# Masks as matmuls, zero matmuls in waits, and new engine orders in a fused attention and channel-mix kernel

## The chip, the cores and the metric

The kernel runs on one core of one Trainium2 chip. The core has five engines: TensorE (PE, with its weight loads listed as PEld), VectorE (DVE), ScalarE (ACT), GpSimd (POOL) and SyncE (SP), which here issues nearly all DMAs. The metric is the device time of one execution in microseconds (us). Several executions of a kernel are timed and the median is taken.

## The reference

Inputs are q, k and v, each 4 batches x 8 heads x 768 positions x 64, in fp32, and the weights of a channel mix. First comes attention in which a query sees the first 4 positions (the sinks) and the last 128, itself included:

```python
scores = scale * q @ k.T
keep = (pos[None] < 4) | ((rel >= 0) & (rel < 128))    # rel = query position - key position
a = softmax(where(keep, scores, -1e9)); x = a @ v      # heads side by side: 512 wide
xk = mu_k * x + (1 - mu_k) * x_prev                    # x_prev: the position before
xr = mu_r * x + (1 - mu_r) * x_prev
out = sigmoid(xr @ w_r) * (relu(xk @ w_k) ** 2 @ w_v)
```

The channel mix follows: w_k is 512 x 1024, w_v 1024 x 512 and w_r 512 x 512. The output is 4 x 768 x 512 in fp32.

## The kernel before

The work is cut into 12 units, each 256 positions of one batch, so three units to a batch. A unit goes through four stages. `prepare` loads q, k and v, casts them to bf16, transposes q and k (on PE with a copy out of PSUM by ACT or DVE, for late units by DMA) and puts v beside a column of ones. `attend` multiplies keys by queries into one of two PSUM tiles called `sc`, takes the exponential on ACT into `e` (line 1092; for unit 0, line 805), multiplies `e` by a mask of zeros and ones on DVE (line 1106; for unit 0, line 818), multiplies by v on PE (lines 1125 and 831) and divides by the sum that the column of ones has made. The sinks, where they lie outside the unit's own keys, have scores and products of their own (lines 987, 1063 and 1078; 1078 is the form in quarter tiles and 1063 the plain one). `mix` transposes x and makes xk and xr on DVE (line 1220; for unit 0, line 907). `ffn` makes the keys (line 1275; for unit 0, line 930, since unit 0 goes in two halves of 128 positions), relu and square, the gate with w_r (line 1314, tanh in place of the sigmoid) and the product with w_v (line 1334). The weights come in fp32 and are cast in pieces: w_k in four, w_r in two, w_v in four (lines 629, 633 and 635).

Nothing of this is ordered by a loop. Each step is entered with `P.op` under a running number, with the keys that it reads and writes and the buffers that it takes or holds. `ORDER` lists the numbers for PE, DVE, ACT, POOL and SP, each engine in the order in which it is to work, and `CHOICE` says for steps that several engines can do which one does them. `Plan.schedule` walks the five lists with planned costs, hands out buffers (four PSUM banks called `bank`, two `sc` tiles, and so on) and puts out the instructions. An engine works through its own list in order; between engines, semaphores hold an instruction until its data is there. A step whose number stands behind another's on the same engine can't pass it.

Two further parts matter here. `Plan.fill` (line 1358) puts matmuls of zeros on PE where the plan sees a wait: over 600 ns in the first 4 us of the plan and over 300 ns after, up to a planned time of 22 us, into a free `bank`; they compute nothing that is used. And `BIAS` names units whose mask is added to the scores by a matmul (a bias of 0 or -30000, times the identity, started in PSUM ahead of the scores) instead of being multiplied on DVE. It is empty, and only the units after unit 0 have the code for it (`biased` in `attend`). The bias tiles would lie in the third output buffer, which is free early, beside the rows of mu. mu is transposed by one small matmul (`spread_mu`, line 614), entered ahead of all units.

Of the kernel before, what the change touches and what calls it, by code (L numbers as in the profile page):

```python
# [8 lines left out]
FP32 = mybir.dt.float32  # L9
# [9 lines left out]
    79: "POOL", 80: "ACT", 81: "ACT", 84: "ACT", 87: "ACT", 91: "DVE", 94: "DVE", 95:  # L19
    "DVE", 97: "DVE", 100: "DVE", 129: "POOL", 132: "DVE", 138: "POOL", 141: "DVE",  # L20
    142: "DVE", 160: "PE/tiles", 172: "PE/full", 177: "ACT", 189: "POOL", 192: "POOL",
    194: "DVE", 198: "DVE", 214: "ACT", 222: "ACT", 225: "DVE", 242: "PE/tiles", 254:
    "PE/full", 271: "POOL", 274: "POOL", 276: "DVE", 283: "DVE", 303: "ACT", 307:
    "ACT", 311: "ACT", 349: "POOL", 352: "DVE", 355: "POOL", 357: "DVE", 361: "DVE",
    381: "ACT", 389: "ACT", 405: "PE/full", 417: "PE/tiles", 433: "POOL", 435: "POOL",
    457: "ACT", 465: "ACT", 469: "ACT", 485: "PE/tiles", 495: "ACT", 497: "PE/full",
    508: "DVE", 510: "DVE", 513: "POOL", 524: "DVE", 540: "ACT", 548: "ACT", 581:
    "ACT", 587: "POOL", 592: "POOL", 594: "DVE", 598: "ACT", 600: "DVE", 616: "ACT",
    620: "ACT", 624: "ACT", 644: "PE/tiles", 656: "PE/full", 667: "POOL", 669: "DVE",
    676: "DVE", 685: "DVE", 698: "ACT", 706: "ACT", 722: "PE/tiles", 732: "ACT", 734:  # L30
    "PE/tiles", 745: "DVE", 749: "DVE", 751: "DVE", 781: "ACT", 808: "ACT", 814:
    "ACT", 819: "ACT", 822: "POOL", 824: "POOL", 826: "DVE", 845: "ACT", 848: "DVE",
    849: "ACT", 853: "ACT", 857: "ACT", 873: "PE/tiles", 883: "ACT", 885: "PE/full",
    890: "ACT", 896: "POOL", 898: "DVE", 902: "POOL", 904: "DVE", 905: "DVE", 925:
    "ACT", 929: "ACT", 933: "ACT", 949: "PE/tiles", 959: "ACT", 961: "PE/full", 980:
    "DVE", 1000: "DVE", 1001: "ACT", 1016: "DVE", 1025: "ACT",
# [7 lines left out]
BIAS = ()  # L44
# [12 lines left out]
FIRST = 0  # L57

# [39 lines left out]
    ),  # L98
    "DVE": (
# [23 lines left out]
    ),  # L123
    "ACT": (
# [15 lines left out]
    ),  # L140
    "POOL": (
# [3 lines left out]
    ),  # L145
# [1274 lines left out]
```

## Time and profile before

| | |
|---|---|
| three timed runs | 167.68, 169.44 and 171.79 us; median 169.44 |
| the profiled execution | 170.43 us, of which the span from first to last instruction is 167.5 |
| mean granted TensorE clock in it | 0.98 |
| DMA | 34.38 MB, mean 205 GB/s |

The profile is of one execution. Its page gives busy time by engine, the span in 40 slices, the chain of work that ended last, groups of instructions with the idle time before them, and DMA issues with the time to landing. Other views of the same trace are used below: busy time by stretches that one chooses (PE, PEld, DVE, ACT and POOL, then the granted clock, the DMA share and GB/s), and the timeline, whose rows have start, duration, engine, line, operation, out<-in, shapes and count, and in brackets the idle time ahead and what ended it. L930 is line 930 of the kernel before. Durations overlap a little when instructions of one engine follow each other, so start-to-start distances are shorter than durations.

### The profile page before, as it was taken

How to read it: one execution, taken by the hardware profiler on the slowest of the kernel's cores; microseconds unless marked ns; L12 is line 12 of the kernel's file. 1: busy time of each engine (PE TensorE's matmuls, PEld its weight loads, DVE VectorE, ACT ScalarE, POOL GpSimd, SP SyncE). 2: the span in 40 equal slices, each digit the busy share in tenths (PEclk: the TensorE clock that was granted, in tenths of full speed). 3: DMA queues.
4: the chain of work that ended last, by engine and by line, in shares of the span. 5: the costliest groups of instructions: out<-in, count | busy, mean ns of one | idle time of the engine just before them, and what ended most of it. 6: DMA issues, size and time to landing. Idle time of an engine off the chain costs nothing.

```text
span 167.5 us, 4800 instructions
## 1 busy us (share of the span) xinstructions
PE 154.5 (92%) x1872; PEld 104.3 (62%) x1890; DVE 145.9 (87%) x373; ACT 133.2 (80%) x246; POOL 36.7 (22%) x66
## 2 busy tenths in 40 slices
PE   6577769999999999999999999999988999999992
PEld 2336559765658676667666686855844774867441
DVE  6499997999899999999999999999949889897241
ACT  3577996999899998999999999799887698522411
POOL 5553202217206133055001320140131000000000
PEclk9997896999999999999999999999999999999999
DMA  4999999995989989999899988989997990302033
GB/s 120 242 306 379 331 304 345 386 388 158 223 245 283 193 214 281 200 210 164 211 178 232 223 197 111 265 155 150 266 136 165 219 224 0 129 0 114 11 129 121
DMA packets 73429, 34.38 MB, mean 205 GB/s; under 512 B 63800, under 2 KB 65088, under 8 KB 73408
## 3 DMA queue, kind: packets, MB, share of 16 engines
q1 hardware_dynamic: 73248, 34.02, 85.9%
q8 instruction: 14, 0.23, 0.6%
q10 hardware_dynamic: 160, 0.07, 0.1%
q14 instruction: 7, 0.06, 0.1%
HBM read 24.12 MB, written 6.29 MB: 182 GB/s over the span
## 4 chain that ended last, share of the span: by engine, by line
PE 68%; DVE 17%; DMA 8%; issue 2%; ACT 2%; SPq 1%; DVEq 0%
PE bank L1334 20%; PE bank L1275 18%; PE bank L1314 11%; PE bank L1125 6%; DMA xt<-x 5%; PE sc L1018 4%; DMA ks<-in_k_dram 3%; DVE e L1106 3%; PE bank L1182 2%; DVE xk L1220 2%; PE bank L706 2%; DVE xk L907 2%; DVE e L818 1%; DVE xr L1220 1%; SPq L476 1%
## 5 line engine op out<-in xcount | busy, mean ns | idle before, releaser
L1334 PE MATMUL bank<-wv_h,kk 128*128 128x512 bf16 x173 | 45.3, 379 | 1.4 <-DVE x L1143 0.8
L1275 PE MATMUL bank<-xk,wk_sb 128*128 128x256 bf16 x352 | 45.8, 273 | 0.2
L1092 ACT ACTIVATE e<-sc 128x1024 bf16<-128x1024 f32 (+1 forms) x44 | 41.5, 977 | 0.1
L1275 PEld LDWEIGHTS <-wk_sb 128*128 128x128 bf16 x352 | 32.8, 98 | 8.1 <-issue 0.9
L1106 DVE TENSOR_TENSOR e<-e,mask 128x1024 bf16<-128x1024 bf16 (+1 forms) x44 | 29.1, 678 | 0.6 <-ACT e L1092 0.6
L1285 ACT ACTIVATE rl<-bank 128x512 bf16<-128x512 f32 x41 | 23.5, 607 | 7.2 <-PE bank L1275 7.1
L1334 PEld LDWEIGHTS <-kk 128*128 128x128 bf16 x184 | 16.9, 98 | 16.1 <-issue 1.1
L744 POOL CAST vb<-vs 128x512 bf16<-128x512 f32 x18 | 14.4, 805 | 44.1 <-DMA vs<-in_v_dram 43.9
L1314 PE MATMUL bank<-wr_sb,xr 128*128 128x512 bf16 x89 | 23.7, 379 | 0.4
L1322 ACT ACTIVATE th<-bank 128x512 f32<-128x512 f32 x24 | 14.5, 613 | 9.5 <-PE bank L1314 9.5
L1220 DVE SCALAR_TENSOR_TENSOR xr<-td,mu_all,xt 128x256 bf16<-128x256 bf16 x44 | 21.8, 506 | 0.0
L1220 DVE SCALAR_TENSOR_TENSOR xk<-td,mu_all,xt 128x256 bf16<-128x256 bf16 x44 | 20.3, 492 | 0.2
L1345 DVE SCALAR_TENSOR_TENSOR ob<-th,bank 128x512 f32<-128x512 f32 x23 | 15.6, 681 | 4.7 <-PE bank L1334 3.1
L1125 PE MATMUL bank<-vb,e 128*128 128x65 bf16 x328 | 15.6, 197 | 0.3 <-DVE vb L744 0.2
L1125 PEld LDWEIGHTS <-e 128*128 128x128 bf16 x328 | 13.8, 100 | 3.1 <-issue 0.3
L1298 ACT ACTIVATE kk<-rl 128x512 bf16<-128x512 bf16 x25 | 15.4, 637 | 0.0
L1314 PEld LDWEIGHTS <-xr 128*128 128x128 bf16 x96 | 8.9, 98 | 9.2 <-issue 0.2
L1143 DVE TENSOR_TENSOR x<-bank,rec 128x256 bf16<-128x256 f32 x34 | 13.8, 415 | 0.4
L1209 DVE TENSOR_TENSOR td<-xt 128x512 bf16<-128x512 bf16 x22 | 9.5, 430 | 3.0 <-DMA xt<-x 2.7
L1018 PE MATMUL sc<-qt,kt 64*64 64x128 bf16 (+2 forms) x480 | 12.0, 229 | 0.0
L1152 ACT ACTIVATE x<-bank,rec 128x64 bf16<-128x64 f32 x40 | 9.2, 322 | 2.9 <-DVE rec L1139 2.8
L1018 PEld LDWEIGHTS <-kt 64*64 64x64 bf16 x480 | 8.7, 109 | 2.7 <-issue 1.5
(104 smaller groups left out, 194.5 us busy)
## 6 DMA issues: line engine op xcount, KB each, us to landing
vs<-in_v_dram SPq DMA_DIRECT2D x24, 256.0 KB, 4.5
out_dram<-ob SPq DMA_DIRECT2D x23, 256.0 KB, 3.0
ks<-in_k_dram SPq DMA_DIRECT2D x16, 256.0 KB, 4.5
qs<-in_q_dram SPq DMA_DIRECT2D x7, 512.0 KB, 5.8
qs<-in_q_dram SPq DMA_DIRECT2D x10, 256.0 KB, 4.5
ks<-in_k_dram SPq DMA_DIRECT2D x4, 512.0 KB, 10.0
w<-in_moe_w_k_dram SPq DMA_DIRECT2D x2, 1024.0 KB, 9.9
w<-in_moe_w_v_dram SPq DMA_DIRECT2D x2, 1024.0 KB, 9.5
```

The lines of the kernel that those rows point to most:

```text
L1018: nc.tensor.matmul(out=sc[keys, a, o0 + f0 - q0:o0 + f1 - q0], lhsT=lhs[rows, keys], rhs=qs[rows, f0:f1], start=u not in BIAS, stop=True, ...
L1092: nc.scalar.activation(out=buf[ek][:, :, lo:], in_=buf[sck][:, :, lo:], func=AF.Exp, scale=scale)
L1106: nc.vector.tensor_tensor(out=at, in0=at, in1=m, op=ALU.mult)
L1125: nc.tensor.matmul(out=o[:, g, a, :], lhsT=e[:, a, e0:e0 + 128], rhs=rhs, start=(T == 0 and i == 0), stop=(i == len(blocks) - 1), skip_gro ...
L1220: nc.vector.scalar_tensor_tensor(out=buf[key][:, c, :], in0=buf[tk][:, i, :], scalar=mu[w][:, c:c + 1], in1=xt[:, c, t0 - 1:t0 + 255], op0 ...
L1275: nc.tensor.matmul(out=ps[:, i, :], lhsT=wk_sb[:, c, 128 * f:128 * f + 128], rhs=xk[:, c, :], start=(c == 0), stop=(c == NC - 1), skip_gro ...
L1285: nc.scalar.activation(out=buf[rk], in_=buf[psk].rearrange("p (i t) -> p i t", i=2), func=AF.Relu)
L1298: nc.scalar.activation(out=buf["kk", u][:, 2 * f2:2 * f2 + 2, :], in_=buf[rk], func=AF.Square)
L1314: nc.tensor.matmul(out=buf[psk], lhsT=buf["xr", u][:, c, 128 * g:128 * g + 128], rhs=wr_sb[:, c, :], start=(c == 0), stop=(c == NC - 1))
L1322: P.op("ACT", act(512), lambda psk=psk, tk=tk: nc.scalar.activation(out=buf[tk], in_=buf[psk], func=AF.Tanh, scale=0.5), rank + 4 + g, tak ...
L1334: nc.tensor.matmul(out=buf[psk], rhs=wv_h[:, f, :], lhsT=buf["kk", u][:, f, 128 * g:128 * g + 128], start=(f == 0), stop=(f == NF - 1))
L1345: P.op("DVE", dve(512), lambda psk=psk, tk=tk, bk=bk: nc.vector.scalar_tensor_tensor(out=buf[bk], in0=buf[tk], scalar=1.0, in1=buf[psk], o ...
```

## The change

`BIAS` becomes `(0, 1)`: the masks of units 0 and 1 are added to their scores by matmuls, and `attend_first` gets the code for it (six matmuls 128x512 for unit 0; eight for unit 1 by the code that was there). POOL makes the two bias tiles. `spread_mu` and its copy are entered behind the scores of unit 0. The identity is kept in fp32 as a whole. The zero matmuls may now go into `sc` tiles and into the buffer that the waiting step itself has taken, and up to a planned time of 36 us. `CHOICE` and `ORDER` are new throughout: 14 matmuls are added on PE, and 13 zero matmuls stand where 5 stood. Of the 24 casts of v, POOL keeps 10 of 18, DVE has 6 for 5 and ACT 8 for 1; DVE has 10 relus for 4. In the order of loads q of unit 0 now leads k, and the first part of w_k goes ahead of q of unit 2, the second behind v of unit 1 and k of unit 2. `STRAIGHT`, a path without the cast, is empty, so its code makes no instruction.

```diff
-BIAS = ()
+BIAS = (0, 1)
...
-    ident8 = tile1([2 * NC, 2 * NC], FP32, "ident8")
+    ident32 = tile1([128, 128], FP32, "ident32")
+    ident8 = ident32[0:2 * NC, 0:2 * NC]
...
             if o["engine"] == "PE" and self.fill:
 
                 now = before
-                while t - now > (300.0 if now > 4000.0 else 600.0) and now < self.fill_until:
-                    some = [b for b in free["bank"] if b[0] <= now]
+                while now < self.fill_until:
+                    least = 300.0 if now > 4000.0 else 600.0
+                    some = [(max(b[0], now), k, name, b) for name in ("bank", "sc") for k, b in
+                            [(1, b) for b in free[name]] + [(0, b) for n, b in own if n == name]]
+                    some = [x for x in some if t - x[0] > least]
                     if not some:
                         break
...
+                    if u in BIAS:
+
+                        def biased(g=g, sk=sk):
+                            w = 128 * (g + 1)
+                            for a in range(2):
+                                nc.tensor.matmul(
+                                    out=buf[sk][:, a, :].rearrange("p (c w) -> p c w", w=w),
+                                    lhsT=ident, start=True, stop=False, skip_group_check=True,
+                                    rhs=bias[0][:, 128 * g:128 * g + w].unsqueeze(
+                                        1).to_broadcast([128, 512 // w, w]))
+
+                        P.op("PE", 430.0, biased, r, lag=PE_LAG, take=[("sc", sk)],
+                             reads=["ident", "bias0"], writes=[sk + ("b",)])
...
-                P.op("DVE", 2 * dve(width // 2, 0.52), masked, r, hold=[ek], port=True,
-                     writes=[part], reads=["mask0"])
+                if u not in BIAS:
+                    P.op("DVE", 2 * dve(width // 2, 0.52), masked, r, hold=[ek], port=True,
+                         writes=[part], reads=["mask0"])
...
+    def after_scores():
+        P.op("PE", 100.0, spread_mu, -40, lag=PE_LAG, take=[("bank", "mup")], mode=4,
+             reads=["ident", ("mu8", 0), ("mu8", 1), ("sc", 0, 0)], writes=["mup"])
+        P.op("DVE", 80.0, lambda: nc.vector.tensor_copy(out=mu_all, in_=buf["mup"][:, 0:2 * NC]), -40,
+             hold=["mup"], reads=["mup"], writes=[("mu", 0), ("mu", 1)])
...
-    P.fill_until = 22000.0
+    P.fill_until = 36000.0
```

More of the change, by code (lines that the diff above doesn't have):

```diff
@@ L18 @@
 CHOICE = {
[L19 to L36, printed above, removed]
+    79: "POOL", 80: "ACT", 81: "POOL", 82: "ACT", 84: "ACT", 87: "ACT", 89: "DVE", 91:
@@ new lines @@
+    "DVE", 92: "DVE", 98: "DVE", 100: "DVE", 102: "ACT", 127: "ACT", 130: "DVE", 132:
+    "DVE", 133: "POOL", 136: "POOL", 141: "DVE", 142: "DVE", 143: "DVE", 145: "DVE",
+    152: "DVE", 162: "PE/full", 173: "PE/full", 181: "ACT", 182: "DVE", 185: "POOL",
+    188: "POOL", 194: "ACT", 195: "DVE", 197: "DVE", 204: "DVE", 213: "ACT", 216:
+    "DVE", 217: "ACT", 220: "DVE", 241: "PE/full", 253: "PE/full", 258: "ACT", 264:
+    "DVE", 270: "POOL", 273: "POOL", 282: "DVE", 289: "DVE", 298: "ACT", 302: "ACT",
@@ new lines @@
+    310: "ACT", 348: "DVE", 351: "DVE", 354: "POOL", 358: "ACT", 360: "DVE", 384:
+    "ACT", 388: "ACT", 404: "PE/full", 416: "PE/tiles", 427: "DVE", 432: "POOL", 434:
+    "POOL", 456: "ACT", 464: "ACT", 484: "PE/tiles", 496: "PE/full", 501: "ACT", 507:
+    "POOL", 509: "POOL", 512: "POOL", 514: "POOL", 517: "ACT", 523: "DVE", 530: "DVE",
+    539: "ACT", 543: "ACT", 551: "ACT", 574: "ACT", 586: "POOL", 588: "POOL", 591:
+    "POOL", 596: "ACT", 597: "ACT", 619: "ACT", 643: "PE/tiles", 655: "PE/full", 666:
@@ new lines @@
+    "POOL", 668: "DVE", 670: "POOL", 672: "DVE", 675: "DVE", 684: "DVE", 693: "ACT",
+    701: "ACT", 721: "PE/tiles", 726: "ACT", 733: "PE/tiles", 746: "POOL", 750:
+    "POOL", 752: "DVE", 776: "ACT", 780: "ACT", 784: "ACT", 813: "ACT", 819: "POOL",
+    823: "POOL", 827: "ACT", 828: "DVE", 844: "ACT", 847: "DVE", 851: "DVE", 852:
+    "ACT", 856: "ACT", 872: "PE/tiles", 884: "PE/full", 889: "ACT", 894: "ACT", 895:
+    "POOL", 899: "DVE", 901: "POOL", 904: "ACT", 923: "DVE", 924: "ACT", 928: "ACT",
@@ L37 @@
+    948: "PE/tiles", 958: "ACT", 960: "PE/full", 970: "ACT", 972: "DVE", 991: "DVE",
+    996: "ACT", 999: "DVE", 1000: "ACT", 1016: "ACT", 1019: "DVE", 1023: "DVE", 1027:
+    "DVE",
 }
@@ L57 @@
 FIRST = 0
+STRAIGHT = ()
 OCT = range(1, 12)
@@ L258, in schedule @@
             lines[o["engine"]].pop(0)
+            own = []
             for name, key in o["take"]:
@@ L261, in schedule @@
                 free[name].remove(b)
+                own.append((name, b))
                 where[key] = b[1]
@@ L303, in schedule @@
                 now = before
-                while t - now > (300.0 if now > 4000.0 else 600.0) and now < self.fill_until:
-                    some = [b for b in free["bank"] if b[0] <= now]
+                while now < self.fill_until:
[3 more added lines that the diff above has]
+                    some = [x for x in some if t - x[0] > least]
                     if not some:
                         break
-                    b = min(some)
-                    free["bank"].remove(b)
+                    now, shared, name, b = min(some)
                     one = 225.0 if now > 4000.0 else 430.0
@@ L312, in schedule @@
                     now += wide * one
-                    free["bank"].append((now, b[1]))
-                    order.append(("fill", self.pools["bank"][b[1]], wide))
+                    if shared:
+                        free[name].remove(b)
+                        free[name].append((now, b[1]))
+                    tile = self.pools[name][b[1]]
+                    order.append(("fill", tile[:, 0, :] if name == "sc" else tile, wide))
             order.append(i)
@@ L478, in load_first @@
                 in_=src[0, :, 128 * g:128 * g + 128, :].rearrange(
-                    "(i h) (p j) d -> p i h (j d)", j=4, h=2)), rank, service=1000.0,
+                    "(i h) (p j) d -> p i h (j d)", j=4, h=2)), rank, service=1400.0 if g else 900.0,
                 descs=272, take=[] if g else [(name + "s", key)], hold=[key] if g else [],
@@ L560, in make_ident @@
         keep(ident, 0, [[1, 128]], -1, ident)
-        nc.gpsimd.tensor_copy(out=ident8, in_=ident[0:2 * NC, 0:2 * NC])
+        nc.gpsimd.tensor_copy(out=ident32, in_=ident)
     def window_mask(out, in_, fill):
@@ L600, in make_sinks @@
             nc.gpsimd.tensor_copy(out=t[:, :, D:D + 1], in_=hmask[:, :, D:D + 1])
-    const_op("POOL", 750.0, make_ident, ["ident"], ["ones0"], rank=-60)
+    const_op("POOL", 900.0, make_ident, ["ident"], ["ones0"], rank=-60)
     if 0 in BIAS:
@@ L614, in spread_mu @@
         nc.tensor.transpose(out=buf["mup"][:, 0:2 * NC], in_=rows8, identity=ident8)
-    P.op("PE", 100.0, spread_mu, -40, lag=PE_LAG, take=[("bank", "mup")], mode=4,
-         reads=["ident", ("mu8", 0), ("mu8", 1), ("sc", 0, 0)], writes=["mup"])
-    P.op("DVE", 80.0, lambda: nc.vector.tensor_copy(out=mu_all, in_=buf["mup"][:, 0:2 * NC]), -40,
-         hold=["mup"], reads=["mup"], writes=[("mu", 0), ("mu", 1)])
     def cast(out, name, i, cut, rank, writes):
@@ L682, in cast @@
                     in_=buf[raw][:, hs, :, :])
-            P.op("ACT", act(512) + 22.0, cast(nc.scalar.copy), rank + half,
-                 alts={"ACT": (act(512) + 22.0, cast(nc.scalar.copy), False),
-                       "DVE": (dve(512, 0.52), cast(nc.vector.tensor_copy), True),
-                       "POOL": (650.0, cast(nc.gpsimd.tensor_copy), True)},
-                 take=[] if half else [(name + "b", rk)],
-                 hold=[raw] + ([rk] if half else []),
-                 reads=[(name, u, half), "table"],
-                 writes=[rk + (half,)])
+            straight = (u, half) in STRAIGHT
+            second = half and (u, 0) not in STRAIGHT
+            if not straight:
+                P.op("ACT", act(512) + 22.0, cast(nc.scalar.copy), rank + half,
+                     alts={"ACT": (act(512) + 22.0, cast(nc.scalar.copy), False),
+                           "DVE": (dve(512, 0.52), cast(nc.vector.tensor_copy), True),
+                           "POOL": (650.0, cast(nc.gpsimd.tensor_copy), True)},
+                     take=[] if second else [(name + "b", rk)],
+                     hold=[raw] + ([rk] if second else []),
+                     reads=[(name, u, half), "table"],
+                     writes=[rk + (half,)])
             if by_dma(name, u):
@@ L700, in prepare, with transpose_straight @@
                 continue
+            def transpose_straight(half=half, psk=psk, raw=raw):
+                src = quarters(buf[raw], half) if u == FIRST else octets(
+                    buf[raw])[:, :, 4 * half:4 * half + 4, :]
+                for j in range(4):
+                    for a in range(2):
+                        nc.tensor.transpose(
+                            out=buf[psk][64 * a:64 * a + 64, 128 * j:128 * j + 128],
+                            identity=ident32, in_=src[:, a, j, :])
             def transpose(half=half, psk=psk, rk=rk, name=name):
@@ L713, in transpose, with turned, evacuate @@
                         in_=buf[rk][:, j % 2, 2 * c:2 * c + 2, :].rearrange("p a d -> p (a d)"))
-            P.op("PE", 225.0, transpose, rank + half, lag=PE_LAG, take=[("bank", psk)],
-                 reads=["ident", rk + (half,)], writes=[psk], hold=[rk])
-            def evacuate(copy, half=half, psk=psk, key=key, name=name):
+            if straight:
+                P.op("PE", 870.0, transpose_straight, rank + half, lag=PE_LAG,
+                     take=[("bank", psk)], reads=["ident", (name, u, half)], writes=[psk],
+                     hold=[raw])
+            else:
+                P.op("PE", 225.0, transpose, rank + half, lag=PE_LAG, take=[("bank", psk)],
+                     reads=["ident", rk + (half,)], writes=[psk], hold=[rk])
+            def turned(psk, straight=straight):
+                return buf[psk] if straight else buf[psk].bitcast(BF16)[:, 0:512]
+            def evacuate(copy, half=half, psk=psk, key=key, name=name, turned=turned):
                 if u == FIRST:
@@ L721, in evacuate @@
                         out=buf[key][:, :, half, :].rearrange("p c (t j) -> p c t j", j=4),
-                        in_=buf[psk].bitcast(BF16)[:, 0:512].rearrange(
-                            "p (j t c) -> p c t j", j=4, c=NP))
+                        in_=turned(psk).rearrange("p (j t c) -> p c t j", j=4, c=NP))
                 if octet(name, u):
@@ L727, in evacuate @@
                             "p c (t j) -> p c t j", j=8)[:, :, :, 4 * half:4 * half + 4],
-                        in_=buf[psk].bitcast(BF16)[:, 0:512].rearrange(
-                            "p (j t c) -> p c t j", j=4, c=NP))
+                        in_=turned(psk).rearrange("p (j t c) -> p c t j", j=4, c=NP))
                 return lambda: copy(
@@ L785, in scores @@
                         nc.tensor.matmul(out=buf[sk][:, a, o0:o0 + 128], lhsT=kt[rows, c, i, :],
-                                         rhs=qt[rows, c, g, :], start=True, stop=True)
+                                         rhs=qt[rows, c, g, :], start=u not in BIAS, stop=True,
+                                         skip_group_check=u in BIAS)
         for g in range(2):
@@ L796, in attend_first @@
                     cs = (2 * cp, 2 * cp + 1) if g else range(4)
+                    if u in BIAS:
+                        def biased(g=g, sk=sk):
+                            w = 128 * (g + 1)
+                            for a in range(2):
+                                nc.tensor.matmul(
[5 more added lines that the diff above has]
+                             reads=["ident", "bias0"], writes=[sk + ("b",)])
                     P.op("PE", 220.0, lambda g=g, cs=cs, sk=sk: scores(g, cs, sk), r,
-                         lag=PE_LAG, mode=1, take=[("sc", sk)], hold=[("kt", u), ("qt", u)],
-                         writes=[sk], reads=[(n, u, i) for n in ("kt", "qt")
+                         lag=PE_LAG, mode=1, take=[] if u in BIAS else [("sc", sk)],
+                         hold=[("kt", u), ("qt", u)] + ([sk] if u in BIAS else []),
+                         writes=[sk], reads=([sk + ("b",)] if u in BIAS else []) + [(n, u, i) for n in ("kt", "qt")
                                              for i in range(g + 1) if (n, i) != ("qt", 0) or not g])
@@ L867, in attend_first @@
                      writes=[("x", u, g, cp)])
+        after_scores()
     def mix_first(u, rank):
```

140 rows, old and new, of the table ORDER are left out of this document.

## The prediction

> **What bounds the kernel now.** I read the page first (shares, then the chain), then busy time by long stretches, then by stretches cut where the granted TensorE clock changes, then the timeline of the first 42 us.
>
> ```profile
> span 167.5 us, 4800 instructions
> PE 154.5 (92%) x1872; PEld 104.3 (62%) x1890; DVE 145.9 (87%) x373; ACT 133.2 (80%) x246; POOL 36.7 (22%) x66
> ```
> ```profile
> 0.00:30.00 30.00, 22.32 (x284) 16.10 (x284) 24.68 (x77) 21.71 (x37) 11.48 (x32) 0.89 0.96 292
> 30.00:50.00 20.00, 19.70 (x253) 12.71 (x256) 19.34 (x44) 18.95 (x33) 5.48 (x9) 1.00 0.89 276
> 50.00:100.00 50.00, 49.55 (x681) 35.16 (x684) 49.30 (x127) 48.52 (x88) 14.66 (x18) 1.00 1.09 215
> ```
>
> Columns: PE, PEld, DVE, ACT and POOL busy, the granted clock, the DMA share, GB/s. From 30 us on PE has hardly a gap (19.70 of 20, 49.55 of 50), so the end comes sooner only by what PE reaches sooner at 30 to 40 us, or by small gaps closed later. PE's 7.7 idle us before 30, and its slow clock there, are what there is to win. DVE and ACT are nearly as full after 30, so a lead lasts only if they share it.
>
> ```profile
> 11.07:14.48 3.41, 1.77 (x33) 1.30 (x33) 3.38 (x11) 2.56 (x5) 1.94 (x5) 1.00 1.03 399
> 14.48:17.90 3.42, 3.35 (x49) 2.65 (x48) 3.24 (x12) 3.15 (x7) 1.34 (x2) 0.50 1.13 332
> 17.90:21.31 3.41, 2.42 (x59) 1.74 (x52) 3.41 (x11) 3.41 (x6) 0.39 (x1) 1.00 1.12 341
> 21.31:24.72 3.41, 1.86 (x36) 1.44 (x34) 3.41 (x8) 3.41 (x6) 0.00 (x0) 1.00 1.09 297
> 24.72:28.14 3.42, 3.42 (x48) 3.41 (x47) 2.61 (x10) 2.56 (x8) 1.40 (x2) 0.50 1.10 344
> ```
>
> Two stretches of 3.4 us run at half clock. Each follows one in which PE was busy 52% or 54%; after the one at 71% the clock stayed whole. DVE is full from 11 to 25 us, the DMA engines throughout.
>
> **The change, part by part.**
>
> *Masks leave DVE.* Units 0 and 1 no longer multiply by a mask:
>
> ```profile
> L818 DVE TENSOR_TENSOR e<-e,mask 128x256 bf16<-128x256 bf16 (+1 forms) x8 | 3.2, 450 | 0.0
> L1106 DVE TENSOR_TENSOR e<-e,mask 128x1024 bf16<-128x1024 bf16 x7 | 4.7, 677 | 0.0
> ```
>
> That is 3.2 us and four of the seven 0.677 us masks (the list is of the first 40 us), 2.7 us: 5.9 us less on DVE, and one step less between exponential and values. The new engine choices hand DVE other work; up to the first product with W_v I count about 1.7 us net (casts, evacuations of x, one relu, less evacuations of q and k). DVE is relieved of about 4.2 us, so the next late thing is looked for on ACT, which gets the casts of v and q and the evacuations that DVE gave up.
>
> *Masks enter PE.* 14 matmuls of 128x512, six for unit 0 and eight for unit 1. Four of this form take 0.86 us in the chain:
>
> ```profile
> 31.25 2.56 PE bank L1275 x22
> ...
> 35.53 0.24 PE bank L1078 x8
> ...
> 38.44 0.98 PE bank L1314 x4
> 39.42 0.86 PE bank L1334 x4
> ...
> 41.40 0.36 PE bank L1063 x4
> ```
>
> So 0.215 each, 3.0 us together. One pair (0.43) stands directly ahead of unit 0's first scores; the rest lie where PE waits for exponentials anyway. Without that cover it would be 3.0.
>
> *Zero matmuls*, 13 where there were 5: three fp32 128x512 (two at the very start), three fp32 128x256, seven bf16 128x512.
>
> ```profile
> 8.79 1.08 PE L1363 MATMUL bank<-warm 128*128 128x512 f32 x2
> ...
> 26.09 1.04 PE L930 MATMUL bank<-xk,wk_sb 128*128 128x128 bf16 x8
> ...
> 28.62 0.61 PE L930 MATMUL bank<-xk,wk_sb 128*128 128x128 bf16 x8
> ```
>
> One fp32 128x512 is at most 1.08, a 128x256 about half. Past the start they sum to 1.08 + 3 x 0.54 + 7 x 0.215 = 4.2 us. If each fits its wait they cost 0; if none does, 4.2. I take 0, as in the stretches they fill PE stands idle for more than that (1.6 us and 1.5 us in the two that precede the drops, more earlier). What they buy: eight products take 1.04 us at half clock and 0.61 at full, and PE in the second slow stretch is on the chain; at most half of 3.42, 1.7 us there. That is no term of its own below: it is inside the way from unit 1's last exponential to its keys.
>
> *Transpose of mu.* One matmul and a copy of 8 columns, moved behind the first scores; before, it stood ahead of the first k transposes and waited for the identity. mu is first needed for unit 0's mix, later in both: 0.
>
> *POOL* builds two further masks early (six small instructions) and casts both halves that it has of W_k; it loses half of its casts of v. Its slack covers that until W_k.
>
> *SP.* q leads k, W_k's first half passes q of unit 2, its second half falls behind v of unit 1 and k of unit 2, and W_r passes a half of v.
>
> ```profile
> w<-in_moe_w_r_dram SPq DMA_DIRECT2D x1, 1024.0 KB, 10.4
> ```
> ```profile
> 9.14 1.44 POOL L744 CAST vb<-vs 128x512 bf16<-128x512 f32 x2 [2.48 <-DMA vs<-in_v_dram]
> ...
> 18.12 4.13 SPq L493 DMA_DIRECT2D w<-in_moe_w_r_dram  x1
> 22.93 3.52 SPq L493 DMA_DIRECT2D w<-in_moe_w_v_dram  x2
> ```
>
> W_r landed at 18.12 + 10.4 = 28.5, and the bytes ahead of it do not grow: 28.5 bounds it from above, and less the half of v that it passes (0.26 MB at the 292 GB/s of the first 30 us, 0.9 us) I take 27.6. W_k's second half, a megabyte (some 3 us) before it, lands at 24 to 25.5. The bytes through W_v's first half and unit 2's v also stay the same, so about 32.4 (22.93 + the 9.5 that the page has for W_v) bounds that v.
>
> *The path, along ACT's queue.* These rows give the spacing of instructions back to back, start to start:
>
> ```profile
> 15.50 1.09 ACT L725 COPY qt<-bank 128x512 bf16<-128x512 bf16 x2
> ...
> 17.90 1.03 ACT L1092 ACTIVATE e<-sc 128x1024 bf16<-128x1024 f32 x1
> ...
> 26.09 0.93 ACT L1152 ACTIVATE x<-bank,rec 128x64 bf16<-128x64 f32 x4 [0.25 <-DVE rec L1139]
> ...
> 30.89 1.07 ACT L629 ACTIVATE wr_sb<-w 128x1024 bf16<-128x1024 f32 x1
> 31.84 1.95 ACT L1092 ACTIVATE e<-sc 128x1024 bf16<-128x1024 f32 x2
> 33.65 1.61 ACT L1285 ACTIVATE rl<-bank 128x512 bf16<-128x512 f32 x3
> 35.08 1.16 ACT L1322 ACTIVATE th<-bank 128x512 f32<-128x512 f32 x2
> 36.16 1.94 ACT L1092 ACTIVATE e<-sc 128x1024 bf16<-128x1024 f32 x2
> 37.99 1.06 ACT L629 ACTIVATE wv_h<-w 128x1024 bf16<-128x1024 f32 x1
> 38.94 0.62 ACT L673 CAST kb<-ks 128x512 bf16<-128x512 f32 x1
> 39.45 0.60 ACT L1322 ACTIVATE th<-bank 128x512 f32<-128x512 f32 x1
> ```
>
> Weight cast 0.95, exponential 0.91, relu 0.48, tanh 0.54, 512-wide cast 0.51, evacuation 0.53, four scalings of x 0.87; estimates are 0.52 for a square (as wide as the cast) and 0.27 for the small exponential (256 of 1024 columns, with a little start).
>
> In the changed order, q of unit 1 lands some 1.4 us behind the first half of v (9.1), at 10.5. ACT then has its cast, two exponentials, an evacuation of q and the cast of v: 10.6 + 0.51 + 1.82 + 0.53 + 0.6 = 14.1. Values, a reciprocal, the k transposes and one evacuation bring 15.6, x of unit 0 brings 16.5, and unit 1's first exponential starts there (17.90 before). Then ACT is full: two exponentials, W_k, q, and relu not before 20.0 (its products need that W_k cast), small exponential, evacuation, exponential, evacuation, exponential: 20.0 + 0.48 + 0.27 + 0.53 + 0.91 + 0.53 + 0.91 = 23.6.
>
> ```profile
> 24.48 0.68 DVE L1106 TENSOR_TENSOR e<-e,mask 128x1024 bf16<-128x1024 bf16 x1
> ```
>
> Before, unit 1's last mask ended at 25.16, and its keys ran steadily from 31.25, 6.1 us later. The same way loses half clock and gains W_r's cast on DVE; I take 5.8: keys from 29.4, with four gate products (0.86) now ahead of them. That is a lead of 31.25 - 29.4 + 0.86 = 2.7 us.
>
> ACT goes on: square, x, evacuation, W_k, evacuation, small exponential reach 27.3; W_r 27.6 to 28.5; relu, exponential, tanh, square, exponential to 31.9; v of unit 2 waits for 32.4 and ends 32.9; two relus, tanh, relu, exponential, relu to 36.3; W_v's last quarter ready at 37.4. PE took the products that need it at 39.42. **Lead 39.42 - 37.4 = 2.0 us.** I take 2.0, as the later point contains the earlier. The ends: 2.7 if that cast is no gate, and 0 if instructions on ACT follow one another at their full durations (1.03 for 0.91, 1.07 for 0.95: about 2 us over these thirty).
>
> PE's own work after that is the same but for two groups of sink products in the plain form (0.36 in the chain for 0.24): 0.2 us, left out. So span 165.5, and with the 2.93 us around it (170.43 - 167.5) 168.4 for this execution. It lies 0.99 above the median 169.44 (runs 167.68 to 171.79), so the median comes to **167.4**.
>
> **The rivals.**
>
> *More than that.* The 2.7 holds, and a later stall also goes:
>
> ```profile
> PE bank L1334 <- DVE x L1143: 0.8, 1, 0.8
> ```
>
> 2.7 + 0.8 = 3.5, so 165.9. For: all orders are new and DVE is relieved. Against: nothing in the change aims at that place.
>
> *The clock drops all the same.* If new stretches end below some 55% again, PE runs its dense part after 24 us at half clock: four groups of eight keys at 0.43 extra are 1.7 us, so 169.1. Against it, by the order and these durations PE has 12.7 us of work in the 15.3 from 14.1 to 29.4.
>
> ```profile
> 13.29 0.69 PE L881 MATMUL bank<-ident,x 128*128 128x128 bf16 x4 [0.76 <-DVE x L848]
> ```
>
> PE's waits ahead of the first drop were of this size, 0.76 us. The Trainium skill, TensorE: Matmul & The Clock Gate, section "Why this matters for your kernels", asks only for no idle gaps over about 3 us. By that rule these short waits need no filling, the zero matmuls buy nothing, and the time would be this rival's; the trace disagrees, since the clock fell after waits under 1 us.
>
> *Slower: casts of v stall ACT.* On POOL they waited for nothing but their data, at no cost:
>
> ```profile
> POOL vb L744 <- DMA vs<-in_v_dram: 43.9, 11, 13.7
> ```
>
> Eight of the 24 casts of v are ACT's now, one before. ACT takes its work in order, so a v that lands after its turn holds the exponentials and relus behind it. With seven more, a stall of 0.29 us each uses up the 2.0, and from there the kernel is slower; at 0.5 each it is 167.4 + 3.5 = 170.9, which I take for this case, and at 0.8 each 173.0. For: the mean POOL wait was 4 us. Against: ACT's turns were placed later, and the one cast it had did not wait.
>
> **How the numbers follow.** Forecast 0.52 (its own range 166.2 to 168.6), more 0.18, clock 0.14, v on ACT 0.16. The range 165.4 to 170.9 leaves out the far ends of the first and last. About 2% is what a measurement of this kernel can tell from no change: below 166.05 lie two thirds of "more" and a little of the forecast, 0.17; above 172.8 a third of the last and some unforeseen wait, 0.09; the rest 0.74.
>
> **What would show it.** Right: no half-clock stretch before 30 us; no masks of units 0 and 1 on DVE; unit 1's first exponential near 16.5, its keys from about 29.4, the first product that needs W_v's last quarter near 37.4; PE full after that. Wrong: PE waiting at 30 to 40 us on ACT or on weights; ACT idle on v's landing; a zero matmul still running when its successor's data is there.

## The result, and the profile after

| | median, us | runs, us | ratio to before, 95% interval |
|---|---|---|---|
| before | 169.25 | 167.26 to 173.38 (20) | |
| changed | 169.86 | 168.77 to 171.43 (20) | 1.0066 [1.0039, 1.0093] |

The forecast was 167.4, a gain of 1.2%, and the kernel became 0.7% slower. That is less than the 2% named in the prediction, but its interval does not reach 1. Ratios here leave out executions more than 1.5% above the fastest of their kernel, and medians take all. The profiled execution of the changed kernel took 169.64 us, close to the median, with a span of 167.9. Before's profiled execution was a long one, 170.43, but 2.9 us of it lie around the span, where most executions have 1.7 to 2.0; its span of 167.5 is close to the median span of 76 further executions of before (167.25), so the two spans can be compared.

The head of the page of the changed kernel, then its busy time by the stretches that the prediction used (PE, PEld, DVE, ACT, POOL, clock, DMA share, GB/s):

```profile
span 167.9 us, 4855 instructions
PE 158.1 (94%) x1906; PEld 104.2 (62%) x1906; DVE 145.4 (87%) x368; ACT 130.4 (78%) x243; POOL 36.8 (22%) x71
```
```profile
0.00:30.00 30.00, 25.21 (x304) 16.23 (x305) 22.02 (x69) 19.97 (x37) 12.52 (x36) 1.00 0.97 295
30.00:50.00 20.00, 20.00 (x252) 12.83 (x250) 19.36 (x49) 19.86 (x37) 4.76 (x7) 1.00 0.97 276
50.00:100.00 50.00, 48.73 (x677) 34.26 (x676) 48.74 (x116) 46.37 (x84) 14.60 (x21) 1.00 1.16 215
```

The clock column is whole now (0.89 before) and DVE does 2.7 us less before 30 us (4.2 were counted up to the first product with W_v). But PE was busy for 0.8 us less between 50 and 100 (48.73 for 49.55), and at the start something new stands. These are rows of the timeline of the changed kernel, of DVE, PE and ACT:

```profile
2.68 0.31 DVE L563 MEMSET sc<- 64x128 f32 x2
```
```profile
2.90 3.78 PE L1414 MATMUL sc<-warm 128*128 128x512 f32 x4 [2.90 <-DVE sc L563]
6.48 1.06 PE L837 MATMUL sc<-ob,ident 128*128 128x512 bf16 x2
7.33 0.61 PE L728 MATMUL bank<-ident,qb 128*128 128x128 bf16 x4
```
```profile
7.98 0.59 ACT L750 COPY qt<-bank 128x512 bf16<-128x512 bf16 x1 [5.09 <-PE bank L728]
...
10.34 1.08 ACT L854 ACTIVATE e<-sc 128x512 bf16<-128x512 f32 x2 [1.25 <-PE sc L819]
```

The two zero matmuls of the start (four rows in the trace) now write a score tile. DVE clears a corner of the score tiles, as the last of its early clearings, and PE has to wait for that: the zeros begin at 2.90, where in before their like, in a bank, began at 1.13:

```profile
1.13 2.93 PE L1363 MATMUL bank<-warm 128*128 128x512 f32 x4 [1.13 <-DVE warm L1383]
```

PE takes its work in order, so the first bias products stand behind the zeros to 6.48, the first transposes to 7.33, and ACT waits 5.09 us for them. Further on, the marks of the path (ACT, then PE, and at last the row of before's timeline for the same products with W_v):

```profile
18.76 1.96 ACT L1143 ACTIVATE e<-sc 128x1024 bf16<-128x1024 f32 x2
```
```profile
31.63 2.78 PE L1326 MATMUL bank<-xk,wk_sb 128*128 128x256 bf16 x24
...
37.27 1.02 PE L1385 MATMUL bank<-wv_h,kk 128*128 128x512 bf16 x4
38.13 1.03 PE L1365 MATMUL bank<-wr_sb,xr 128*128 128x512 bf16 x4
39.00 1.03 PE L1385 MATMUL bank<-wv_h,kk 128*128 128x512 bf16 x4
```
```profile
39.25 1.03 PE L1334 MATMUL bank<-wv_h,kk 128*128 128x512 bf16 x4
```

Unit 1's first exponential is at 18.76 (forecast 16.5, before 17.90), the keys at 31.63 (29.4, 31.25), W_v's last quarter at 39.00 (forecast 37.4). The 39.42 of the prediction is where the chain has before's products; in the chain a piece begins where the one ahead of it ends. In the timeline, as for the changed kernel, they begin at 39.25. So 0.25 us of the lead of 2.0 were there, and PE's waits between 40 and 165 us take more than that:

```profile
PE bank L1114 <- DVE ob L1396: 0.7, 1, 0.7
PE bank L1365 <- DVE x L1194: 0.4, 1, 0.4
PE bank L1176 <- DVE e L1157: 0.3, 1, 0.3
PE bank L1176 <- DVE ob L1396: 0.2, 1, 0.2
```

L1176 waits at 53 to 54 us, L1114 at 77 and L1365 at 140. Together they are 1.6 us, where before had one wait of 0.8, at L1334, which is gone. From W_v's last quarter to the end of the span before took 128.2 us and the changed kernel 128.9, and the end comes 0.4 us later.

### The profile page after: what moved, and what is told of

It reads as the page before. It is cut to its first block, busy times and chain, and to the rows that moved or that the text cites. A ratio compares the mean times of both kernels' runs of the same rounds, so it can differ in the third digit from the quotient of the medians.

```text
span 167.9 us, 4855 instructions
## 1 busy us (share of the span) xinstructions
PE 158.1 (94%) x1906; PEld 104.2 (62%) x1906; DVE 145.4 (87%) x368; ACT 130.4 (78%) x243; POOL 36.8 (22%) x71
## 5 line engine op out<-in xcount | busy, mean ns | idle before, releaser
L1385 PE MATMUL bank<-wv_h,kk 128*128 128x512 bf16 x184 | 46.7, 379 | 0.0
L1143 ACT ACTIVATE e<-sc 128x1024 bf16<-128x1024 f32 (+1 forms) x44 | 42.1, 986 | 1.6 <-PE sc L1069 1.4
L1157 DVE TENSOR_TENSOR e<-e,mask 128x1024 bf16<-128x1024 bf16 (+1 forms) x40 | 26.8, 685 | 0.2 <-ACT e L1143 0.2
L1336 ACT ACTIVATE rl<-bank 128x512 bf16<-128x512 f32 x36 | 21.4, 620 | 5.9 <-PE bank L1326 5.3
L1385 PEld LDWEIGHTS <-kk 128*128 128x128 bf16 x184 | 16.7, 98 | 13.7
L1365 PE MATMUL bank<-wr_sb,xr 128*128 128x512 bf16 x96 | 24.5, 379 | 0.4 <-DVE x L1194 0.4
L1373 ACT ACTIVATE th<-bank 128x512 f32<-128x512 f32 x24 | 15.0, 626 | 10.1 <-PE bank L1365 10.0
L1271 DVE SCALAR_TENSOR_TENSOR xk<-td,mu_all,xt 128x256 bf16<-128x256 bf16 x44 | 21.2, 500 | 0.2
L772 POOL CAST vb<-vs 128x512 bf16<-128x512 f32 x10 | 8.2, 825 | 40.2 <-DMA vs<-in_v_dram 36.9
L1176 PE MATMUL bank<-vb,e 128*128 128x65 bf16 x328 | 15.3, 193 | 0.8 <-DVE e L1157 0.3
L1176 PEld LDWEIGHTS <-e 128*128 128x128 bf16 x328 | 13.3, 97 | 4.1 <-DVE e L1157 0.4
L1365 PEld LDWEIGHTS <-xr 128*128 128x128 bf16 x96 | 9.0, 98 | 9.0 <-issue 0.6
L687 POOL CAST kb<-ks 128x512 bf16<-128x512 f32 x10 | 7.2, 720 | 20.9 <-DMA ks<-in_k_dram 12.9
```

The lines of the kernel that those rows point to most:

```text
L1143: nc.scalar.activation(out=buf[ek][:, :, lo:], in_=buf[sck][:, :, lo:], func=AF.Exp, scale=scale)
L1157: nc.vector.tensor_tensor(out=at, in0=at, in1=m, op=ALU.mult)
L1176: nc.tensor.matmul(out=o[:, g, a, :], lhsT=e[:, a, e0:e0 + 128], rhs=rhs, start=(T == 0 and i == 0), stop=(i == len(blocks) - 1), skip_gro ...
L1271: nc.vector.scalar_tensor_tensor(out=buf[key][:, c, :], in0=buf[tk][:, i, :], scalar=mu[w][:, c:c + 1], in1=xt[:, c, t0 - 1:t0 + 255], op0 ...
L1336: nc.scalar.activation(out=buf[rk], in_=buf[psk].rearrange("p (i t) -> p i t", i=2), func=AF.Relu)
L1365: nc.tensor.matmul(out=buf[psk], lhsT=buf["xr", u][:, c, 128 * g:128 * g + 128], rhs=wr_sb[:, c, :], start=(c == 0), stop=(c == NC - 1))
```

## The experiments

The theory tried first (A): the prediction's path is right, but the start is late, because the zero matmuls wait for a clearing. Its rivals: the start has slack, and the masks as matmuls, the zero matmuls further on or the later orders cost it. When A was settled, two more stood against each other: C, that the lead is given back at three waits for DVE, and D, that DVE is full and a wait taken away comes back elsewhere. The table has the median and the ratio to executions of before that were timed together with it (12 executions each, 6 of e2, e3 and e6):

| kernel | us | ratio, 95% interval |
|---|---|---|
| e1, start's zeros in banks | 168.01 | 0.9948 [0.9905, 0.9991] |
| e2, zeros only in the first 4 us | 170.69 | 1.0122 [1.0061, 1.0184] |
| e3, masks on DVE again | 176.80 | 1.0453 [1.0392, 1.0514] |
| e4, before with the new zeros | 169.13 | 0.9987 [0.9936, 1.0037] |
| e5, score tiles cleared first | 168.30 | 0.9915 [0.9876, 0.9954] |
| e6, e1 and three moves on DVE | 166.80 | 0.9865 [0.9810, 0.9920] |
| e7, e1 without the start's zeros | 169.83 | 1.0099 [1.0048, 1.0150] |
| e8, changed kernel and the moves | 169.25 | 0.9972 [0.9926, 1.0018] |
| e9, e6 without the start's zeros | 169.12 | 1.0013 [0.9964, 1.0062] |
| e10, e6, zeros only in the first 4 us | 167.95 | 0.9950 [0.9903, 0.9998] |

**e1.** The changed kernel, but zero matmuls of the first 4 us only in banks.

```diff
                             [(1, b) for b in free[name]] + [(0, b) for n, b in own if n == name]]
+                            if now > 4000.0 or name == "bank"]
```

> The changed kernel, but its zero matmuls of the first 4 us go into banks, which nothing has to clear, and not into the score tiles, which DVE clears at 2.68 to 2.99 us. Theory A (the start is what failed): in the changed kernel the first zero matmul started at 2.90 us behind that clearing, not at 1.13, and four halves of 0.85 us kept PE until 6.48, so the first transposes came at 7.33 and unit 1's first exponential at 18.76 instead of the 16.5 that I had forecast. Then here the zeros start near 1.1, the transposes near 5, unit 1's exponential near 16.7, the first product with W_v's last quarter near 37.5 (39.00 in the changed kernel), and the time is 1.3 to 2.0 us below the changed kernel's 169.9, about 168.2. Theory B (the loads and ACT gate at 30 to 40 us anyway, and the new order's own stalls at 53, 77 and 140 us, 2.3 us together, eat the rest): unit 1's exponential comes earlier, but the product with W_v's last quarter no earlier than 38.5, and the time stays at 169.4 to 170.0.

168.01, 1.85 us under the changed kernel (1.2% by the ratios), and a little faster than before: A. The zeros begin at 1.13 as in before:

```profile
1.13 3.67 PE L1415 MATMUL bank<-warm 128*128 128x512 f32 x4 [1.13 <-DVE warm L1435]
4.63 0.60 PE L838 MATMUL sc<-ob,ident 128*128 128x512 bf16 x2
5.07 0.39 PE L729 MATMUL bank<-ident,qb 128*128 128x128 bf16 x4
```

The zeros were released 1.77 us sooner (2.90 less 1.13), and the time fell by about as much. Not all marks came where A put them: in the profiled execution, at 169.38 longer than the median, unit 1's first exponential is at 17.77 (16.7 expected) and W_v's last quarter at 37.84 (37.5), since PE had to wait for a q that POOL casts:

```profile
PE bank L729 <- POOL qb L684: 1.7, 1, 1.7
```

**e2.** The changed kernel without the zero matmuls after 4 us: `P.fill_until = 4000.0` for `36000.0`.

> The changed kernel without its zero matmuls after the first 4 us (11 of 13 left away; the two at the start stay). If the zeros hold the clock, a stretch of 3.4 us at half clock comes back between 11 and 28 us and the time rises by 0.5 to 1.5 us, to 170.4 to 171.4. If they stand on the path instead (one of them ran at 8.00 to 9.30 ahead of unit 0's second half), the time falls by up to 0.5. If neither, unit 1's first exponential stays at 18.8 and the time within 0.4 of 169.9.

0.8 us slower than the changed kernel, with intervals that overlap. So these zeros are no cost; that they earn something is likely, but not shown. In the profiled execution the clock fell once before 30 us, with no idle gap of PE over 0.93 us ahead of it:

```profile
7.65:11.07 3.42, 2.22 (x26) 1.42 (x25) 1.60 (x3) 1.82 (x4) 1.06 (x3) 1.00 1.06 328
11.07:14.48 3.41, 2.99 (x30) 1.86 (x30) 1.27 (x6) 1.47 (x4) 2.65 (x10) 0.54 1.04 368
```

That execution, of 173.55, is the longest of the six (mean clock 0.99). The other five have 0.997 to 1.0, so such a drop does not explain their median of 170.66.

**e3.** The changed kernel with the masks of units 0 and 1 multiplied on DVE right behind each exponential, and without the 14 bias matmuls.

```diff
+                    m = m.rearrange("p k q -> p (k q)").unsqueeze(1).to_broadcast([128, 2, w])
+                    for a in range(2):
+                        at = buf[ek][:, a, cols].rearrange("p (c w) -> p c w", w=w)
+                        nc.vector.tensor_tensor(out=at, in0=at, in1=m, op=ALU.mult)
```

> The changed kernel with the masks of units 0 and 1 back on DVE, directly behind each exponential, and without the 14 matmuls of the masks; orders, zeros and loads as changed. By my forecast's first step (5.9 us of DVE on the way to unit 1's keys) the time rises by 2 us or more, to about 172. If DVE has room by then (it was busy 7.4 of 10 us from 10 to 20 and 9.4 from 20 to 30), only the step between exponential and values counts, some 0.7 us a unit, and the time is 170.3 to 171. If the matmuls cost as much as they save, it is within 0.4 of 169.9.

6.9 us slower than the changed kernel. The masks as matmuls are a part without which the new orders do not hold. The figure is not the price of the masks alone: neither DVE's order nor the zeros' places were planned for masks on DVE, and its clock fell too (0.89 before 30 us in its profile, 0.91 from 30 to 50). That these matmuls cost the gain is refuted.

**e4.** Before with the changed kernel's rule for zero matmuls, up to 36 us, in the first 4 us in banks.

> The kernel before with the changed rule for zero matmuls alone (also in score tiles and in the step's own buffer, to 36 us of the plan; in the first 4 us in banks only). If the half-clock stretches at 14.5 to 17.9 and 24.7 to 28.1 cost time, they go, and the time falls by 0.7 to 1.7 us, to 167.6 to 168.5. If DVE sets the pace there, or the added zeros stand ahead of work, the clock is whole but the time is within 0.5 of 169.25 or above it.

The half clock was gone (1.00 in all stretches of its profile up to 31 us, and at least 0.996 on average in every execution) and the time the same. That does not show that the half clock was free. Of the 76 executions of before that were timed beside e1 to e10, 24 had a mean clock of at least 0.992, and their median span is 166.3 us; 31 had 0.985 to 0.992, with 167.5; 21 had less, with 168.4. So a lower clock went with a longer time, though which of the two brought the other is not shown. e4, with its clock whole, has a median span of 167.4. The reading that fits both is that added zeros which stand ahead of work cost about what the whole clock brings; no run separates the two.

**e5.** The changed kernel, with DVE's clearing of the score tiles ahead of its other clearings; the zeros stay in the score tile.

> The changed kernel, in which only the order of VectorE's clearings is other: the score tiles are cleared first, not last, so that the zero matmuls in a score tile are released at about 1.5 us and not at 2.9. Theory A (the changed kernel lost its gain because its zero matmuls at the start were released late): they end 1.3 to 1.5 us earlier, unit 0's first exponential comes at about 9.0 instead of 10.34, and the time is 168.4 to 168.9, nearly as low as where they stand in banks (168.0). Rival B (it is not the late release but the tile, a score buffer held over the zeros): 169.5 to 170.2, as the changed kernel.

168.30, 1.6 us under the changed kernel (1.5% by the ratios). It is the time of release, not the tile:

```profile
1.32 3.78 PE L1414 MATMUL sc<-warm 128*128 128x512 f32 x4 [1.32 <-DVE sc L557]
4.89 1.06 PE L837 MATMUL sc<-ob,ident 128*128 128x512 bf16 x2
```

Unit 0's first exponential came at 8.97, as expected, although the first bias products still ran at half speed (1.06, against 0.60 in e1).

**e6.** e1 with three moves in DVE's order. PE's order stays the same; the plan hands out some other banks.

```diff
-294, 336, 341, 321
+336, 341, 321, 294
...
-668, 498, 479
+668, 479, 498
...
-952, 914, 920, 953
+952, 914, 953, 920
```

294 is a mix of x, 336, 341 and 498 are masks, 321 and 479 output products (`ob`), 920 a square, 953 a scaling of x.

> The kernel with the zero matmuls of the start in banks (168.0), with three moves in VectorE's order alone: a mix of x for the gate behind two masks and the output product that the tensor engine waited for at 53 to 54 us; the output product ahead of a mask at 77 us; a scaling of x ahead of a square at 140 us. Theory C (the lead of 1 to 2 us is given back at these three waits, 0.6 + 0.8 + 0.4 us): they go and the time is 166.6 to 167.4. Rival D (VectorE is full there, so that a move only shifts the wait to the next late thing): 167.8 to 168.3, with waits of the same sum at other places.

166.80, the best here, and 2.6 us under the executions of before that were timed with it (169.44). C: between 40 and 165 us PE's list of waits now has one row.

```profile
PE bank L1327 <- DVE x L1195: 0.3, 1, 0.3
```

**e7.** e1 without zero matmuls in the first 4 us.

> The changed kernel without any zero matmul in the first 4 us (those after that stay). Theory A: no work stands in the way of the first transposes, so the time is at or under that with the zeros in banks, 167.7 to 168.3, unless the clock is half for longer: then 168.5 to 169.2. Rival (the start does not matter): 169.5 to 170.2.

Against theory A: 169.83. That lies in the range of the rival, that the start does not matter, but e1 and e5 have refuted this rival. In the profiled execution the bias products were free to start at 3.95, as soon as POOL had made the identity, so in the changed kernel the zeros held them back by 2.5 us:

```profile
3.95 1.03 PE L838 MATMUL sc<-ob,ident 128*128 128x512 bf16 x2 [3.95 <-POOL ident L570]
```

Full speed was there by 7.3 us and unit 1's first exponential at 16.66, as in e6. It fell back after 90 us, where among others POOL waited for a v, and PE for POOL (0.7):

```profile
94.85 1.55 POOL L773 CAST vb<-vs 128x512 bf16<-128x512 f32 x1 [5.99 <-DMA vs<-in_v_dram]
```

From this alone one can't say whether the start's zeros were missed, hence e9.

**e8.** The changed kernel with the three moves of e6, and its late start as it is.

> The changed kernel with the same three moves in VectorE's order and its late start as it is. Theory C: the start and the three waits add up independently, so 168.6 to 169.2, some 0.8 to 1.2 us below the changed kernel. Rival D: 169.5 to 170.0.

169.25, 0.6 us under the changed kernel and just above the range of C; the ratios, which compare executions of one occasion, have 0.9%. By them start and moves add up: the start brings 1.2% without the moves (1.0066 to 0.9948) and 1.1% with them (0.9972 to 0.9865), the moves bring 0.9% and 0.8%. Each of these ratios is known to about 0.5%.

**e9.** e6 without zero matmuls in the first 4 us.

> The kernel with the zeros of the start in banks and the three moves in VectorE's order (166.8), without any zero matmul in the first 4 us. Without those zeros the kernel of before the moves took 169.83 although its start was as early; it fell back at 92 to 142 us. Theory E (that is a matter of the later orders, where casts and loads come late, and the zeros of the start are worth nothing by themselves): its markers up to 80 us stand within 0.3 us of those of the kernel with them, and the time differs from 166.8 only by waits after 90 us, 166.6 to 168.5. Rival F (the zeros of the start are worth about 1.8 us by the clock): 168.4 to 169.0, with slower matmuls and a delay already before 40 us.

169.12: rival F, not E. Its profiled execution shows what the zeros can buy. Without them everything that PE does up to about 11.5 us runs at half speed:

```profile
8.65 0.63 PE L729 MATMUL bank<-ident,kb 128*128 128x128 bf16 x4
9.07 1.06 PE L838 MATMUL sc<-ob,ident 128*128 128x512 bf16 x2
...
12.26 0.59 PE L838 MATMUL sc<-ob,ident 128*128 128x512 bf16 x2
```

The first exponential comes at 10.72 (8.75 in e6), unit 1's first at 19.19 (16.69) and W_v's last quarter at 39.25 (37.07). E was also wrong that the marks up to 80 us would be the same. By the ratios, leaving out the zeros of the start costs 1.5% here (0.9865 to 1.0013) and 1.5% in e7 (0.9948 to 1.0099). In e7's profiled execution, however, full speed came early, so by which way e7 lost its 1.5% stays open.

**e10.** e6 without the zero matmuls after 4 us.

> The same 166.8 kernel with the zero matmuls of the first 4 us alone; those in the waits from 4 to 36 us are left out. By the changed kernel, where their leaving out cost 0.8 us, 167.4 to 167.9, with a half-clock stretch of 3.4 us before 30 us. Rival G (waits under 1 us need no filling): 166.5 to 167.0 and the clock whole throughout.

167.95, 1.15 us above e6, as e2 had 0.8. The medians speak for the zeros after 4 us, but the intervals of e6 and e10 overlap. In the profiled execution, of 166.07 (the shortest of the twelve), the clock column is whole in every stretch up to 31 us, as G has it. Why the others were slower no trace here shows.

## Why the prediction was wrong

*PE bounds it from 30 us, and there is time to win before.* Right. e6 won it, with a mended start and three moves that the change did not have.

*Masks leave DVE.* Right in kind: DVE works 2.7 us less on balance, up to 30 us and also up to 40, where the prediction counted 4.2. By e3 the new orders need it.

*Masks enter PE, one pair on the path, 0.43.* The place was right. In the changed kernel that pair took 1.06 at half speed; in e1 and e6 it took 0.60, and the next matmul began 0.44 and 0.43 after it.

*Zero matmuls: the step that failed.* The prediction priced the zeros "past the start", took 0 for them, and left the two at the very start out of the sum, as if they began at 1.13 like before's, which wait only for their operand. The diff says that they may now go into `sc` tiles, and a tile that another engine clears first is a wait like any other. The release came 1.77 us later; e1 and e5, which take that wait away in two ways, got 1.85 and 1.6 us back. "A zero matmul still running when its successor's data is there" was named as what would make the prediction wrong, and that is what happened, at the very first one: it ran to 6.48, where by e7 the bias products were free at 3.95.

*The path along ACT's queue.* Right, once the start is. In the profiled execution of e6, where the zeros start at 1.13, unit 1's first exponential is at 16.69 (forecast 16.5), the keys at 29.70 (29.4) and W_v's last quarter at 37.07 (37.4), so the spacings of ACT's instructions gave each within 0.35 us, although a v of unit 2, for which the prediction had ACT wait to 32.4, was cast at 32.07 without a wait. The low end of the range was summed too small: full durations, 0.06 to 0.12 longer in the rows shown, make about 3 us over thirty instructions and not 2. Nothing hung on it.

```profile
16.69 1.97 ACT L1144 ACTIVATE e<-sc 128x1024 bf16<-128x1024 f32 x2
```
```profile
29.70 2.78 PE L1327 MATMUL bank<-xk,wk_sb 128*128 128x256 bf16 x24
...
37.07 1.03 PE L1386 MATMUL bank<-wv_h,kk 128*128 128x512 bf16 x4
```

*The lead carries to the end: the second step that failed.* The prediction left PE's work after 40 us out as the same, and so put new waits there at nothing. With its start mended (e1) the kernel's ratio is 0.9948, where the forecast was 0.988, as new waits at 52 to 54, 77 and 140 us eat into the lead. They are worth 0.8% (e6) to 0.9% (e8). With the moves too the lead holds, in the profiled executions 2.2 us at W_v's last quarter (39.25 less 37.07) and 2.9 at the end (span 164.6 for 167.5). The prediction had said that DVE is nearly as full as PE after 30 us, and yet looked for the next late thing on ACT alone. At 77 us DVE's order did a mask ahead of the `ob` that frees PE's bank (changed kernel, DVE):

```profile
75.51 0.83 DVE L687 CAST qb<-qs 128x512 bf16<-128x512 f32 x1
76.26 1.09 DVE L1157 TENSOR_TENSOR e<-e,mask 128x1024 bf16<-128x1024 bf16 x1
77.27 0.68 DVE L1396 SCALAR_TENSOR_TENSOR ob<-th,bank 128x512 f32<-128x512 f32 x1
```

*The rivals.* "The clock drops all the same": not in the clock column of the changed kernel, though the start, which this column does not show, ran at half speed to 7.8 us. Its price of 1.7 us is open, by what stands at e4. Its condition, a stretch busy for less than some 55%, does not hold up: in e1 a stretch of 50%, with a wait of 1.7 us in it, was followed by a clock of 1.00. And a clock that short waits do not drop would leave the forecast as it is; the prediction gave this rival's time for that case, which does not follow.

```profile
11.07:14.48 3.41, 1.72 (x22) 1.19 (x21) 2.35 (x8) 2.38 (x4) 2.05 (x5) 1.00 1.07 372
```

"Casts of v stall ACT": no. ACT waited once for a v, too little to matter:

```profile
ACT vb L772 <- DMA vs<-in_v_dram: 0.4, 1, 0.4
```

"More": the stall at L1334 did go, and others came. The slower side came by a mechanism that was not among the rivals.

## What to carry to other kernels

A filler matmul is free only if the buffer that it writes is ready: it inherits that buffer's wait, and all work behind it in the queue does so too. Give it a buffer that nobody has to prepare, and look at what releases the first instruction of each queue. When an order is new throughout, a lead at 40 us is not yet a lead at the end; list the waits of the bounding engine after the change and mend the two or three longest, as they are cheap (here three pairs of numbers, 0.8 to 0.9%). Here the effects of the start and of the later waits added up, within the noise, on an engine that had hardly a gap between the two.

## What the runs showed of the hardware

The clock column does not show the start. It reads 1.00 up to 7.65 us in every kernel here, while in the changed kernel two bias products take 1.06 us at 6.48 and 0.59 at 9.37; the durations of one form tell the speed. The full speed came at about 4.4 us in e1 and e6 (zeros from 1.13), by 6.3 in e8 (zeros from 2.90), between 6.4 and 7.8 in the changed kernel (also from 2.90), e5 (from 1.32), e7 (no zeros) and e10 (from 1.13), and at about 11.5 in e9 (no zeros). So an early release can bring it early but does not settle it. The Trainium skill, TensorE: Matmul & The Clock Gate, section "What's actually happening", has a free-running window of 3.4 us behind this, so that the moment differs from run to run. It agrees that e10 and e6, the same at the start, differ by 2 to 3 us and e8 and the changed kernel by about 1.5; e7 and e9, the same there but for a wait of 0.59 us for a k in e9, differ by more than 4, which is more than one window.

In the changed kernel a mask 128x1024 on DVE took 0.68 us in most places and 1.09 at 73.70 and at 76.26, where POOL cast at the same time (from 73.45 and, below, from 76.01):

```profile
76.01 0.80 POOL L772 CAST vb<-vs 128x512 bf16<-128x512 f32 x1
```
